# Attention scores of two heads on the two halves of TensorE's rows, in float32

## The chip, the cores and the metric

One core of one Trainium2 chip. The metric is the device time of one execution in microseconds; the kernel before is given by the median of three runs.

## The reference, cut to what matters

Per batch and head (B = 4, H = 8, S = 576, D = 64) a causal attention and a linear memory read are mixed by a gate; the result, 2304 tokens of 512 features, goes through two MLPs, all in float32.

```python
scores = q @ k.T / 8                     # causal
local = softmax(scores) @ v
phi = where(q > 0, q, exp(q) - 1) + 1
mem = (phi @ M_prev) / (phi @ z_prev + 1e-6)
x = g * mem + (1 - g) * local            # g = sigmoid(beta), per head
h = x @ w_in;  x = (h * sigmoid(1.702 * h)) @ w_out
h = x @ w_in2; x = (h * clip(h + 3, 0, 6) / 6) @ w_out2
```

## The kernel before, in words

**Work.** The tokens lie in six tiles of 384 (`TILES`, L73): the first 384 rows of one batch (g = 0), or the last 192 rows of two batches (g = 1), which attend to all 576 keys. Attention goes by pairs of heads, four a segment: 32 pairs, 16 of 384 rows (numbers 0 to 7 and 16 to 23) and 16 of 192 rows. The MLPs (`moe`, L271) hold their weights and the activations split into a float32r part and the rest, also float32r; each product is three full-array matmuls of 384 columns, and one tile takes 16 units of 24 matmuls.

**Stages.** The first tile's attention runs first, with the first weight pieces' conversion (`conv_w`, L188: weights come as float64 and are put together by DVE, POOL and ACT). Then the stream of the first MLP over tiles 0 to 4 has the attention of the next tile mixed in (`pump`, L800): `after_quarter` and the loop at L845 take one step of the attention generator whenever the MLP's count of quarter units passes a rate (L855). The rest of the conversion lies in tile 0's stretch (L854). Last come the first MLP's tile 5 and the whole second MLP without attention. The order on each engine's queue is set at build time by a scheduler from the order in which the code gives the instructions and a simulated timeline; each queue then runs in order. `Chains` (L87) hands out the follow-up steps of softmax, evacuation, gates and conversion one at a time.

**A pair.** `scores` (L464) writes the scores into PSUM banks; `soft` (L473) takes the masked minimum of the negated scores on DVE (L391), exponentials with sums on ACT (L396), the reciprocal on DVE and the scaling on POOL (L404). `turn` (L553) transposes the probabilities on PE and evacuates them. `mem_prep` and `mem_read` (L608, L626) make phi and the memory part. `weigh` (L663) forms the weighted sums with the values, each head on half of the array's columns (64 values' columns as weights), and adds the transposed memory part. Three PSUM banks (tag `a`) go round between all of them once the MLP runs; eight while the first tile's attention runs alone.

**How scores are formed.** Pairs 0 and 2 to 7 are not split: `product` (L436) multiplies float32 q and k, 64 rows of the array for one head, first head 0, then head 1. The others (`is_split`, L369) are split: `split_qk` (L422) loads q and k of one head twice, on both halves of the partitions, and makes the float32r part of q on POOL (L430), that of k on ACT (L431), q's rest on DVE (L433), k's rest on POOL or DVE (L434); the scores are then two full-array float32r matmuls per block. Blocks: 128, 256 and 384 columns a head in a 384-row pair (two banks a head), 512 columns in a 192-row pair; there the last 64 rows of both heads go together as the corner product (L517 to L522), 64x64 of the array each. A float32 matmul stands in the trace as two records (two passes), a transposition as one. In a 192-row pair the last block of sums (L690), the second memory block (L635) and its transposition (L696) use 64 rows or columns.

**Weighted sums of now**, with a step in the middle, at which the MLP can go on:

```python
av(0, lambda a: t[a][:, 0:384], 0, 384, 128, True)
yield
need(("t", i, 0, 1), ("t", i, 1, 1))
av(1, lambda a: t[a][:, 384:640], 128, 384, 128, False)
av(2, lambda a: t[a][:, 640:768], 256, 384, 128, False)
```

Of the kernel before, what the change touches and what calls it, by code (L numbers as in the profile page):

```python
# [8 lines left out]
F32 = mybir.dt.float32  # L9
# [15 lines left out]
KQ = 100  # L25
# [6 lines left out]
SPLIT = (2, 3, 4, 5)  # L32
SP0 = (1,)
KL0 = (1, 1)
SB = 1
RB = 3
T4B = 1
# [12 lines left out]
KLP = (1, 1, 1, 0, 0, 1)  # L50
# [20 lines left out]
GQK = 2 * N0  # L71
# [39 lines left out]
def attention_moe_kernel(ctx: ExitStack, tc: tile.TileContext, qk0, sk0, sk1, vm0, vm1, bb, w1, w2, out):  # L111
# [76 lines left out]
    def conv_w():  # L188

        key = layer, f, a = w_jobs[w_at[1]]  # L190
# [146 lines left out]
    banks = [3, 0]  # L337

    def bank(name):
        k = banks[1] % banks[0]  # L340
        banks[1] += 1
        if k < 3:
            return psa.tile([128, 512], F32, tag="a", bufs=3, name=name)
        return psy.tile([128, 512], F32, tag=("h", "y0", "y1", "y2", "y3")[k - 3], name=name)
# [6 lines left out]

    def at_transpose(*args):
        on_pe[:] = [PE.transpose(*args).ins]  # L353

    def attention(ap):
        qk, vm, pp, pt, phi, mo, raw, sp = {}, {}, {}, {}, {}, {}, {}, {}
        gens = {}
        norms, cut = [0, 0], set()
# [10 lines left out]
        def is_split(i):  # L369
            return pairs[i][0] in SPLIT or i in SP0  # L370

        def load_qk(i):
            if i >= NPAIR or is_split(i):
                return
            ti, si, b, g, p, _ = pairs[i]
            t = ap.tile([128, 2 * N0], F32, tag="raw", bufs=RB, name="qk")
            move(1, out=t[:, 0:GQK], in_=qk0[b, p])
            qk[i] = (t[:, 0:N0], t[:, N0:GQK])

# [15 lines left out]
        def expo(dst, o, m, s):  # L395
            ACT.activation(out=dst, in_=o, func=AF.Exp, scale=-1.0, bias=m, accum_out=s)  # L396
# [12 lines left out]
        def load_raw(i, a):  # L409
            if not 0 <= i < NPAIR or not is_split(i) or (i, a) in raw:  # L410
                return
            ti, si, b, g, p, _ = pairs[i]
            t = ap.tile([128, 2 * N0], F32, tag="raw", bufs=RB, name="raw")
            move(3, out=t, in_=(sk0, sk1)[g][b, 2 * p + a])
            raw[i, a] = t

        def split_start(i, a):
            if (i, a) in raw and (i, a) not in cut:
                cut.add((i, a))
                start(("sp", i, a), split_qk(i, a))  # L420

        def split_qk(i, a):  # L422
            ti, _, _, g = pairs[i][:4]
            nq, nk = ((N0, N0), (N1, S))[g]
            r = raw[i, a]
            t = ap.tile([128, 3 * N0], F32R, tag="sp", bufs=SB, name="sp")
            rq, rk = r[:, 0:nq], r[:, nq:nq + nk]
            q_h, q_l, ks = t[:, 0:nq], t[:, nq:2 * nq], t[:, 2 * nq:2 * nq + nk]
            sp[i, a] = q_h, q_l, ks
            POOL.tensor_scalar(out=q_h, in0=rq, scalar1=1.0, scalar2=1.0, op0=ALU.mult, op1=ALU.mult)  # L430
            ACT.copy(out=ks, in_=rk)  # L431
            yield
            DVE.tensor_tensor(out=q_l, in0=rq, in1=f32(q_h), op=ALU.subtract)  # L433
            (DVE, POOL)[KL0[a] if i < NP else KLP[ti]].tensor_tensor(out=ks[D:128], in0=rk[D:128], in1=f32(ks[D:128]), op=ALU.subtract)  # L434

        def product(i, a):  # L436

            ti, si, b, g, p, _ = pairs[i]
            if not is_split(i):
                q, k = qk[i]  # L440
                h = slice(64 * a, 64 * a + 64)

                def mm(o, c0):
                    n = o.shape[1]
                    at_matmul(o, lhsT=q[h, c0:c0 + 128], rhs=k[h, 0:n], start=True, stop=True)

                return mm, lambda: None

            split_start(i, a)
            need(("sp", i, a))  # L450
            q_h, q_l, ks = sp[i, a]

            def mm(o, c0):
                n = o.shape[1]
                at_matmul(o, lhsT=q_h[:, c0:c0 + 128], rhs=ks[:, 0:n], start=True, stop=False)
                at_matmul(o, lhsT=q_l[:, c0:c0 + 128], rhs=ks[:, 0:n], start=False, stop=True)

            def done():
                sp.pop((i, a))
                split_start(*((i, 1) if a == 0 else (i + 1, 0)))  # L460

            return mm, done

        def scores(i):  # L464
            ti, si, b, g, p, _ = pairs[i]
            norms[1] = ti
            if is_split(i):
                start(("p", i), mem_prep(i))
                load_raw(i + 1, 0)
            st = ap.tile([128, 12], F32, tag="st", name="st")  # L470
            mx, su = st[:, 0:6], st[:, 6:12]

            def soft(s, cols, a, dst, c):  # L473
# [7 lines left out]
                for x, (c0, c1) in enumerate(cols):  # L481
                    expo(dst[:, c0:c1], s[:, c0:c1], mx[:, c + x:c + x + 1], su[:, c + x:c + x + 1])
# [7 lines left out]
            for a in range(2):  # L490
                h = slice(64 * a, 64 * a + 64)
                mm, done = product(i, a)
                if g == 0:
                    t = ap.tile([128, 512], F32, tag="p", bufs=PB, name="p")
                    s = bank("s01")
                    mm(s[:, 0:128], 0)
                    mm(s[:, 128:384], 128)
# [429 lines left out]
```

## Time and profile before

| | us |
|---|---|
| median of three runs | 1102.02 (1100.32 to 1103.64) |
| the profiled execution | 1097.73 |
| its span | 1095.9 |
| PE busy | 1052.0 (96%) |
| DVE busy | 570.7 (52%) |
| ACT busy | 539.1 (49%) |
| POOL busy | 472.1 (43%) |
| granted clock of TensorE, mean | 0.984 |

PE is TensorE's matmul, PEld its weight load, DVE VectorE, ACT ScalarE, POOL GpSimd, SP the queue that issues DMAs. Matmuls are pipelined and a record is longer than the time until the next starts: what a matmul costs is read from start to start. "128*64" in a PE row are the array's rows and columns in use; the shape after it is the moving operand's. "L350" is the line of the helper that records every attention matmul, so the tile names (s scores, o sums, t transposes, mem memory) tell them apart. A wait "<- issue" is time in which the profile shows nothing that the engine waited for.

### The profile page before, as it was taken

How to read it: one execution, taken by the hardware profiler on the slowest of the kernel's cores; microseconds unless marked ns; L12 is line 12 of the kernel's file. 1: busy time of each engine (PE TensorE's matmuls, PEld its weight loads, DVE VectorE, ACT ScalarE, POOL GpSimd, SP SyncE). 2: the span in 40 equal slices, each digit the busy share in tenths (PEclk: the TensorE clock that was granted, in tenths of full speed). 3: DMA queues.
4: the chain of work that ended last, by engine and by line, in shares of the span. 5: the costliest groups of instructions: out<-in, count | busy, mean ns of one | idle time of the engine just before them, and what ended most of it. 6: DMA issues, size and time to landing. Idle time of an engine off the chain costs nothing.

```text
span 1095.9 us, 17060 instructions
## 1 busy us (share of the span) xinstructions
PE 1052.0 (96%) x6153; PEld 958.1 (87%) x6153; DVE 570.7 (52%) x1511; ACT 539.1 (49%) x1225; POOL 472.1 (43%) x526
## 2 busy tenths in 40 slices
PE   7988779999999999999999998998999999999998
PEld 5566667788889999889888997998999999999998
DVE  7899999635766564435445588884111121111210
ACT  6766665544555555435443566765233232332422
POOL 5688867544444435444543344543222222222221
PEclk9989989999999999999999998999999999999999
DMA  7542322212231212212120585101000010000000
GB/s 245 202 184 101 121 82 63 73 58 74 82 106 54 63 40 82 69 48 73 44 63 25 204 294 176 57 1 44 15 29 30 1 59 1 30 29 1 30 1 29
DMA packets 32627, 81.77 MB, mean 75 GB/s; under 512 B 3744, under 2 KB 12960, under 8 KB 32544
## 3 DMA queue, kind: packets, MB, share of 16 engines
q1 hardware_dynamic: 32544, 80.69, 21.9%
q8 instruction: 48, 0.79, 0.3%
q14 instruction: 35, 0.29, 0.1%
HBM read 71.24 MB, written 9.44 MB: 74 GB/s over the span
## 4 chain that ended last, share of the span: by engine, by line
PE 76%; DVE 11%; issue 6%; POOL 5%; ACT 1%; DMA 1%; SPq 0%; POOLq 0%; ACTq 0%; DVEq 0%
PE h L305 10%; PE h L307 10%; PE h L306 10%; PE y L287 10%; PE y L286 10%; PE y L285 10%; PE o L350 6%; PE s L350 5%; PE t L353 3%; POOL r L209 2%; POOL g L268 2%; DVE r L205 2%; DVE r L200 2%; PE mem L350 1%; DVE s L391 1%
## 5 line engine op out<-in xcount | busy, mean ns | idle before, releaser
L268 POOL TENSOR_TENSOR g<-t,g 128x384 fp32r<-128x384 f32 x176 | 183.5, 1043 | 407.7 <-ACT g L266 380.9
L305 PE MATMUL h<-xs,w 128*128 128x384 f32 x768 | 266.9, 348 | 19.8 <-DVE t L259 12.3
L306 PE MATMUL h<-xs,w 128*128 128x384 f32 x768 | 261.1, 340 | 0.3 <-DVE w L228 0.3
L307 PE MATMUL h<-xs,w 128*128 128x384 f32 x768 | 261.1, 340 | 0.3 <-DVE xs L251 0.2
L285 PE MATMUL y<-g,w 128*128 128x384 f32 x768 | 259.1, 338 | 0.6 <-ACT g L266 0.5
L286 PE MATMUL y<-g,w 128*128 128x384 f32 x768 | 257.4, 336 | 0.0
L287 PE MATMUL y<-g,w 128*128 128x384 f32 x768 | 241.4, 339 | 3.1 <-DVE g L268 2.9
L263 DVE SCALAR_TENSOR_TENSOR t<-t,h 128x384 f32<-128x384 f32 x96 | 53.1, 553 | 272.1 <-ACT t L261 272.1
L305 PEld LDWEIGHTS h<-xs,w 128*128 128x128 f32 x768 | 147.2, 192 | 30.3 <-DVE t L259 16.7
L266 ACT CAST g<-t 128x384 fp32r<-128x384 f32 x192 | 98.5, 513 | 111.6 <-DVE t L259 56.8
L287 PEld LDWEIGHTS y<-g,w 128*128 128x128 f32 x768 | 141.4, 188 | 9.1 <-DVE g L268 3.9
L307 PEld LDWEIGHTS h<-xs,w 128*128 128x128 f32 x768 | 146.8, 191 | 1.6 <-DVE xs L251 1.1
L306 PEld LDWEIGHTS h<-xs,w 128*128 128x128 f32 x768 | 147.2, 192 | 1.1 <-DVE w L228 0.6
L285 PEld LDWEIGHTS y<-g,w 128*128 128x128 f32 x768 | 144.7, 188 | 3.2 <-issue 1.0
L286 PEld LDWEIGHTS y<-g,w 128*128 128x128 f32 x768 | 144.5, 188 | 0.3
L261 ACT ACTIVATE t<-h,three 128x384 f32<-128x384 f32 x96 | 55.6, 579 | 169.6 <-PE h L307 169.6
L404 POOL TENSOR_SCALAR p<-p,st,omg 128x128 f32<-128x128 f32 (+2 forms) x128 | 93.4, 737 | 84.3 <-DVE st L400 58.7
L391 DVE CUSTOM_DVE_ANT_0 s<-s,mask 128x128 f32<-128x128 f32 (+2 forms) x144 | 73.8, 519 | 74.7 <-PE s L350 73.5
L396 ACT ACTIVATE p<-s,st 128x128 f32<-128x128 f32 (+3 forms) x160 | 82.9, 524 | 25.7 <-DVE st L391 23.3
L259 DVE SCALAR_TENSOR_TENSOR t<-t,h 128x384 f32<-128x384 f32 x96 | 52.7, 549 | 62.1 <-ACT t L257 59.0
L257 ACT ACTIVATE t<-h 128x384 f32<-128x384 f32 x96 | 47.0, 490 | 61.6 <-PE h L307 54.4
L209 POOL TENSOR_SCALAR r<-r 128x512 f32<-128x512 f32 x64 | 57.1, 895 | 30.5 <-DVE r L205 22.4
(86 smaller groups left out, 1348.2 us busy)
## 6 DMA issues: line engine op xcount, KB each, us to landing
r<-in_w_dram SPq DMA_DIRECT2D x64, 512.0 KB, 5.0
raw<-in_sk_dram SPq DMA_DIRECT2D x50, 384.0 KB, 3.2
vm<-in_vm_dram SPq DMA_DIRECT2D x16, 386.0 KB, 3.0
x2d<-yo SPq DMA_DIRECT2D x24, 192.0 KB, 2.0
xr<-x2d SPq DMA_DIRECT2D x24, 192.0 KB, 3.1
out_dram<-yo SPq DMA_DIRECT2D x24, 192.0 KB, 1.9
vm<-in_vm_dram SPq DMA_DIRECT2D x16, 258.0 KB, 2.8
qk<-in_qk_dram SPq DMA_DIRECT2D x7, 384.0 KB, 3.8
```

The source lines that it names most:

```text
L266: gated["ACT"].append(ACT.copy(out=g[:, 0], in_=t).ins)
L268: d = (DVE, POOL)[GLE[ti if layer == 0 else -1]].tensor_tensor(out=g[:, 1], in0=t, in1=f32(g[:, 0]), op=ALU.subtract)
L285: PE.matmul(ys[d], lhsT=w[:, 0, o:o + 128], rhs=g[:, 0], start=(f == 0), stop=False)
L286: PE.matmul(ys[d], lhsT=w[:, 1, o:o + 128], rhs=g[:, 0], start=False, stop=False)
L287: PE.matmul(ys[d], lhsT=w[:, 0, o:o + 128], rhs=g[:, 1], start=False, stop=(f == NF - 1))
L305: PE.matmul(h, lhsT=w[:, 0, c:c + 128], rhs=x[:, 0], start=(kk == 0), stop=False)
L306: PE.matmul(h, lhsT=w[:, 1, c:c + 128], rhs=x[:, 0], start=False, stop=False)
L307: PE.matmul(h, lhsT=w[:, 0, c:c + 128], rhs=x[:, 1], start=False, stop=(kk == KD - 1))
L350: on_pe[:] = [PE.matmul(out, **args).ins]
L391: DVE.tensor_tensor_reduce(out=o, in0=o, in1=m, scale=-SCALE, scalar=init, op0=ALU.add, op1=ALU.min, accum_out=out)
L396: ACT.activation(out=dst, in_=o, func=AF.Exp, scale=-1.0, bias=m, accum_out=s)
L404: (DVE, POOL)[e[norms[0] % len(e)]].tensor_scalar(out=dst, in0=dst, scalar1=s, scalar2=w, op0=ALU.mult, op1=ALU.mult)
```

## The change

Both heads' scores are formed from float32 q and k for all pairs, head 0 on rows 0 to 63 of the array and head 1 on rows 64 to 127, into two banks, block by block in turns. The matmuls of a bank pair are tied in order, and the first of them is given all waits: for the last readers of both banks (`in_a_run`, `free`, `has_read`). The split of q and k goes, with its buffers and loads; for 192-row pairs each head loads its 64 partitions with a DMA of its own. The weighted sums of a pair, with the memory part's transpositions, become one such run, which waits for all evacuated transposes and the scaled memory part; the step in the middle goes. In 192-row pairs the 64-row remainders are padded to 128: `t4` has zero rows, and the second memory block is rows 64 to 191, whose first 64 get the weight zero (`gall`'s fourth block). A weight piece first finishes the piece four before it. Steps per pair fall from 12 to 9 and from 9.5 to about 7; the rates `KQ` and those in `pump` are set to that.

```diff
-KQ = 100
+KQ = 80
-SPLIT = (2, 3, 4, 5)
-SP0 = (1,)
-SB = 1
+GW = (0, 2)
...
     def conv_w():
-        key = layer, f, a = w_jobs[w_at[1]]
+        n = w_at[1]
+        key = layer, f, a = w_jobs[n]
+        if n >= 4 and w_jobs[n - 4] in w_gen:
+            chains.finish(w_gen[w_jobs[n - 4]])
...
+    def after(ins, deps):
+        for dep in deps:
+            tc.add_manual_dep(
+                ins, dep.name, mybir.DependencyInfo(mybir.DependencyClass.Sync, mybir.DependencyReason.DATA),
+                reason="one run of matmuls",
+            )
+
+    def in_a_run(deps):
+        run = []
+        def mm(out, **args):
+            ins = PE.matmul(out, **args).ins
+            if run:
+                tc.add_manual_dep(
+                    ins, run[-1].name,
+                    mybir.DependencyInfo(mybir.DependencyClass.NoSync, mybir.DependencyReason.DATA),
+                    reason="one run of matmuls",
+                )
+            else:
+                after(ins, deps)
+            run.append(ins)
+            on_pe[:] = [ins]
+        return mm
...
+        t4 = ap.tile([128, 2, 64], F32, tag="t4", bufs=1, name="t4")
+        POOL.memset(t4, 0.0)
...
         def load_qk(i):
-            if i >= NPAIR or is_split(i):
+            if i >= NPAIR:
                 return
...
+            if g == 0:
+                move(1, out=t, in_=qk0[b, p])
+                qk[i] = (t[:, 0:N0], t[:, N0:2 * N0])
+            else:
+                for a in range(2):
+                    h = slice(64 * a, 64 * a + 64)
+                    move(3, out=t[h], in_=sk1[b, 2 * p + a][h])
+                qk[i] = (t[:, 0:N1], t[:, N1:N1 + S])
...
-        def split_qk(i, a):
...
         def scores(i):
+            def product(banks, blocks):
+                mm = in_a_run(free(banks[0]) + free(banks[1]))
+                for o0, o1, c0 in blocks:
+                    for a in range(2):
+                        h = slice(64 * a, 64 * a + 64)
+                        mm(
+                            banks[a][:, o0:o1], lhsT=q[h, c0:c0 + 128], rhs=k[h, 0:o1 - o0], start=True, stop=True
+                        )
...
+            if g == 0:
+                parts = (((0, 128, 0), (128, 384, 128)), ((0, 384, 256),))
+            else:
+                parts = (((0, 512, 0),),)
...
+            for x, blocks in enumerate(parts):
+                s = [bank("s") for _ in range(2)]
+                product(s, blocks)
+                for a in range(2):
+                    gen = soft(s[a], [(o0, o1) for o0, o1, _ in blocks], a, t[a][x], c + 3 * a if g == 0 else a)
+                    start(("s", i, a, x), gen)
+                c += len(blocks)
                 yield
...
         def rows(g):
-            return ((0, 128), (128, 128), (256, 128)) if g == 0 else ((0, 128), (128, 64))
+            return (0, 128, 256) if g == 0 else (0, N1 - 128)
...
         def mem_prep(i):
-            for h, r in q:
-                ACT.activation(out=e[h, 0:n], in_=r, func=AF.Exp)
+            ACT.activation(out=e[:, 0:n], in_=r, func=AF.Exp)
...
         def weigh(i):
+            need(("t", i, 0, 0), ("t", i, 0, 1), ("t", i, 1, 0), ("t", i, 1, 1), ("m", i))
             o = bank("o")
+            mm = in_a_run(list(made.pop(i).values()))
...
+                av(0, lambda a: t[a][:, 0:384], 0, 384, True)
+                av(1, lambda a: t[a][:, 384:640], 128, 384, False)
+                av(2, lambda a: t[a][:, 640:768], 256, 384, False)
             else:
                 for j in range(4):
-                    av(j, lambda a: t[a][:, j], 0, N1, 128, j == 0)
-                    if j == 1:
-                        yield
-                av(4, lambda a: t[2][:, a], 128, N1, 64, False)
+                    av(j, lambda a: t[a][:, j], 0, N1, j == 0)
+                av(4, lambda a: t4[:, a], 128, N1, False)
...
         def gates():
+            POOL.memset(gall[0:64, 3], 0.0)
+            ACT.copy(out=gall[:, 1:3], in_=gall[:, 0:1].to_broadcast([128, 2, H]))
+            ACT.copy(out=gall[64:128, 3], in_=gall[64:128, 0])
...
-                pump((qi - OFF) / (PG0 * 128 / 48 if TILES[ti + 1][0][1] == 0 else PG1 * 128 / 76))
+                pump((qi - OFF) / (PG0 * 128 / 36 if TILES[ti + 1][0][1] == 0 else PG1 * 128 / 57))
```

## Rows read from the trace of the kernel before

**Rows 1.** The page, part 4: chain that ended last, shares of the span by engine.
```profile
PE 76%; DVE 11%; issue 6%; POOL 5%; ACT 1%; DMA 1%; SPq 0%; POOLq 0%; ACTq 0%; DVEq 0%
```
**Rows 2.** Busy time of each engine by stage; the row names its columns.
```profile
core 0: us, PE busy (x) PEld busy (x) DVE busy (x) ACT busy (x) POOL busy (x), PEclk, DMA share, GB/s
0.00:14.00 14.00, 7.72 (x32) 6.43 (x33) 7.85 (x31) 6.94 (x19) 5.94 (x16) 0.90 0.84 300
14.00:57.00 43.00, 41.03 (x208) 23.66 (x207) 38.52 (x161) 32.11 (x99) 28.65 (x39) 0.98 0.59 208
57.00:192.00 135.00, 112.95 (x604) 94.52 (x605) 132.89 (x287) 87.04 (x189) 106.59 (x100) 0.92 0.30 105
192.00:609.00 417.00, 415.37 (x2600) 362.27 (x2601) 220.60 (x767) 208.53 (x539) 181.37 (x228) 1.00 0.21 63
609.00:1096.00 487.00, 474.98 (x2716) 471.28 (x2714) 170.81 (x269) 204.52 (x381) 149.59 (x145) 0.99 0.17 58
```
**Rows 3.** Timeline of PE, third stage: start us, us, engine, line, operation, count.
```profile
302.71 0.33 PE L286 MATMUL y<-g,w 128*128 128x384 f32 x1
302.88 0.34 PE L285 MATMUL y<-g,w 128*128 128x384 f32 x1
303.15 0.87 PE L350 MATMUL o<-pt,vm 128*64 128x192 f32 x8
303.95 0.62 PE L350 MATMUL s<-sp 128*128 128x384 f32 x2
304.50 0.55 PE L350 MATMUL o<-pt,vm 128*64 128x192 f32 x4
```
**Rows 4.** Timeline of PE, second stage: one head's float32 scores on half the rows.
```profile
63.00 0.91 PE L350 MATMUL s<-qk 64*128 64x384 f32 x2
63.84 0.33 PE L350 MATMUL o<-ident,mo 128*128 128x128 f32 x1
```
**Rows 5.** Timeline of PE, third stage: both heads' scores of the corner.
```profile
244.86 1.19 PE L350 MATMUL s<-raw 64*64 64x512 f32 x8
245.99 0.55 PE L353 MATMUL t4a<-ident,p 128*128 128x128 f32 x3
```
**Rows 6.** Groups by line on DVE, 57 to 192 us (busy us, mean ns | idle before).
```profile
L433 DVE TENSOR_TENSOR sp<-raw,sp 128x192 fp32r<-128x192 f32 x8 | 8.1, 1018 | 0.0
L624 DVE SCALAR_TENSOR_TENSOR phi<-raw,phi 64x192 f32<-64x192 f32 x6 | 3.7, 610 | 0.1
```
**Rows 7.** Groups by line on POOL, 57 to 192 us.
```profile
L434 POOL TENSOR_TENSOR sp<-raw,sp 64x576 fp32r<-64x576 f32 x8 | 13.1, 1642 | 0.7
L430 POOL TENSOR_SCALAR sp<-raw 128x192 fp32r<-128x192 f32 x8 | 4.1, 516 | 1.9 <-PE s L350 1.9
```
**Rows 8.** Waits, whole span: us in total, times, longest us.
```profile
PEld o L350 <- issue: 23.8, 103, 0.5
PEld s L350 <- issue: 14.9, 59, 0.6
```
**Rows 9.** Timeline of POOL and PE, first stage: pair 1's split and its scores.
```profile
9.34 0.51 POOL L430 TENSOR_SCALAR sp<-raw 128x384 fp32r<-128x384 f32 x1 [7.29 <-DMA raw<-in_sk_dram]
...
11.35 1.86 PE L350 MATMUL s<-sp 128*128 128x128 f32 x6 [4.96 <-POOL sp L434]
```
**Rows 10.** Groups by line on DVE, 192 to 609 us.
```profile
L433 DVE TENSOR_TENSOR sp<-raw,sp 128x192 fp32r<-128x192 f32 (+1 forms) x40 | 20.3, 507 | 1.8 <-POOL sp L430 1.3
```
**Rows 11.** Timeline of DVE and ACT, third stage: softmax of one head's scores.
```profile
239.56 0.70 DVE L391 CUSTOM_DVE_ANT_0 s<-s,mask 128x512 f32<-128x512 f32 x1 [1.22 <-PE s L350]
...
240.18 0.14 DVE L391 DVE_READ_ACCUMULATOR2_ANT st<- 128x1 f32 x1
...
240.35 0.69 ACT L396 ACTIVATE p<-s,st 128x512 f32<-128x512 f32 x1
```
**Rows 12.** Waits of PE, first 192 to 609 us, then 57 to 192 us.
```profile
PE h L305 <- DVE t L259: 1.3, 2, 1.0
...
PE h L305 <- DVE t L259: 11.0, 5, 4.3
```

More of the change, by code (lines that the diff above doesn't have):

```diff
@@ L70 @@
 BIG = 3.4028234e38
-GQK = 2 * N0
 MZ = 132
@@ L336, in attention_moe_kernel @@
     NPAIR = len(pairs)
-    banks = [3, 0]
+    banks = [3, 0, 0]
+    place = {}
+    last_read = {}
     def bank(name):
@@ L342, in bank, with has_read, free @@
         if k < 3:
-            return psa.tile([128, 512], F32, tag="a", bufs=3, name=name)
-        return psy.tile([128, 512], F32, tag=("h", "y0", "y1", "y2", "y3")[k - 3], name=name)
+            t = psa.tile([128, 512], F32, tag="a", bufs=3, name=name)
+            at = ("a", banks[2] % 3)
+            banks[2] += 1
+        else:
+            tag = ("h", "y0", "y1", "y2", "y3")[k - 3]
+            t = psy.tile([128, 512], F32, tag=tag, name=name)
+            at = (tag, 0)
+        place[id(t)] = at, t
+        return t
+    def has_read(t, d):
+        last_read[place.pop(id(t))[0]] = d.ins
+    def free(t):
+        d = last_read.get(place[id(t)][0])
+        return [] if d is None else [d]
     on_pe = []
@@ L395, in expo @@
         def expo(dst, o, m, s):
-            ACT.activation(out=dst, in_=o, func=AF.Exp, scale=-1.0, bias=m, accum_out=s)
+            return ACT.activation(out=dst, in_=o, func=AF.Exp, scale=-1.0, bias=m, accum_out=s)
         def inverse(s):
@@ L407, in norm @@
             norms[0] += 1
[L409 to L420, printed above, removed]
-        def split_qk(i, a):
[L423 to L431, printed above, removed]
-            yield
[L433 to L462, printed above, removed]
         def scores(i):
@@ L539, in scores, with evac @@
                 yield
-            if is_split(i):
-                need(("p", i))
-                load_raw(i + 1, 1)
-        def evac(jobs):
+        def evac(i, jobs):
             yield
-            for e, out, in_ in jobs:
+            for e, out, in_, *bank_done in jobs:
                 if e is ACT:
-                    ACT.copy(out=out, in_=in_)
+                    d = ACT.copy(out=out, in_=in_)
                 else:
-                    DVE.tensor_copy(out=out, in_=in_)
+                    d = DVE.tensor_copy(out=out, in_=in_)
+                made.setdefault(i, {})[e] = d.ins
+                for t in bank_done:
+                    has_read(t, d)
         def turn(i):
@@ L707, in split @@
                 if XEV[i % len(XEV)]:
-                    DVE.tensor_copy(out=x[:, c:c + n], in_=o[:, 0:n])
+                    d = DVE.tensor_copy(out=x[:, c:c + n], in_=o[:, 0:n])
                 else:
-                    ACT.copy(out=x[:, c:c + n], in_=o[:, 0:n])
+                    d = ACT.copy(out=x[:, c:c + n], in_=o[:, 0:n])
+                has_read(o, d)
             start(("x", i), split())
@@ L726, in attention @@
             load_qk(k)
-            for a in range(2):
-                load_raw(k, a)
             if k == 0:
@@ L745, in attention @@
             if has(i):
-                if not is_split(i):
-                    start(("p", i), mem_prep(i))
+                start(("p", i), mem_prep(i))
                 load_qk(i + 2)
-                if has(i + 1) and is_split(i + 1) and not is_split(i):
-                    for a in range(2):
-                        load_raw(i + 1, a)
             if has(i - 2) and pairs[i - 2][5]:
```

137 lines of the change are left out of this document (47 added, 90 removed).

## The prediction

> **What bounds the kernel now.** I read the table by stage first, then the chain, then PE's timeline at single runs of matmuls, then the queue that is full in each stage. The chain that ended last is 76% PE and 11% DVE [rows 1]; one number for a span with three regimes, so the stages decide [rows 2]. From 0 to 57 us the first tile's attention runs alone: DVE is busy 46.4 of 57 us, PE 48.8. From 57 to 192 us the first tile's MLP, the second tile's attention and the weight conversion run together: DVE is busy 132.9 of 135 us and PE only 113.0, so **DVE bounds this stage**. From 192 to 609 us four MLP tiles run with the rest of the attention: PE 415.4 of 417 us, DVE 220.6: **PE bounds it**. From 609 us on only MLP is left; the change touches nothing there, and I cost those 487 us at no change.
>
> In the third stage the MLP needs 4 x 384 matmuls, which follow each other every 0.17 us (0.1735 over a longer stretch) [rows 3]: 266 us. So 150 us are attention. Its column work by the code, at two columns' time per fp32 pass, two passes (one in a transposition) and 2.4 GHz: a 384-row pair 4.8 us, a 192-row pair 5.2 us. Of the 16 pairs of 192 rows, a quarter's splits lie in the second stage already (8 of 32 instructions, see part 1); counting 13 here, and 8 of 384 rows, makes 106 us. The rest, some 44 us, is above all the price of going into and out of matmuls that use a part of the array. One such run: the MLP matmul at 302.88 holds PE 0.27 instead of 0.17 us before the weighted sums start; those (eight records of 192 columns, two heads side by side: 4 x 0.16 = 0.64 us) take 0.80; then a first full-array matmul pays about 0.1 more [rows 3]. In and out: **0.36 us per run of weighted sums**. For fp32 scores on one half of the rows: 0.84 us where the columns need 0.64 [rows 4], with 0.1 on either side: **0.40 us per run**. The split scores of now are full-array float32r matmuls and pay none of this between MLP matmuls.
>
> **Part 1, scores from float32.** Column time first. Split: two matmuls per head of one column time each; float32: two passes per head of two, but both heads at once if the halves of the rows work side by side. A 384-row pair: 2 x 2 x 768 columns = 4 x 768 = 1.28 us, both ways; a 192-row pair's 512 columns: 0.85 both ways. So split pairs save no columns; the seven unsplit ones (0, 2 to 7), whose heads run one after the other now, halve from 2.56 to 1.28 us.
> Do the halves overlap? No row shows two 64-row matmuls with 128 output columns at once. Nearest: the 64x64 corner pair, both heads, 512 and 64 columns, takes 1.13 us to the next matmul, where overlapped columns need 0.96 and serial ones 1.92 [rows 5]; and the sums on the array's column halves [rows 3]. Both overlap fully, so I take full overlap; serial is the other bound (1.28 and 0.85 us more a pair) and a rival.
> The Trainium skill ("TensorE: Matmul & The Clock Gate", Part 3) measured 3.07 times for four row tiles, not four; two tiles at that efficiency would make a pair's scores some 0.39 and 0.26 us dearer, about 6 us over the third stage (an estimate from that page). The corner pair shows no such loss [rows 5].
> What goes with the split: on DVE the subtraction L433 (8 in the second stage, 8.1 us) and half of phi's instructions L624 (6 of 0.61 us become 3) [rows 6]; on POOL L434 and L430 (13.1 + 4.1 us) [rows 7]; on ACT a cast per head. In the third stage DVE, ACT and POOL have half their time free, so there this is worth nothing.
>
> **Part 2, weighted sums in one run, padded.** By the code a 384-row pair's sums are two runs now, one after. A 192-row pair now leaves full-array mode up to six times: two runs of sums, the 64-row block of sums (another mode), the 64-column memory block, its 64-row transposition, and the corner scores; about 2.0 us with those that touch each other. After: scores, corner scores, sums: 0.40 + 0.36 + 0.36 + 0.05 for a transposition of 128 columns instead of 64 = 1.17 us. That 162 entries into partial modes are seen as drains now (103 and 59) [rows 8] against 96 runs after (64 of scores, 32 of sums) says the same.
>
> **Sum by stage.**
> *0 to 57 us.* Pair 1's scores start at 11.35, held 4.96 us by POOL's split, which began when the halves had landed at 9.34 [rows 9]; without it about 2 us earlier. On PE five unsplit pairs are scored here: 5 x 1.28 = 6.4; ten runs fewer, 4.0; four runs of sums fewer, 1.4; pair 1's two new runs, 0.8 back: 11 us. DVE caps that: it idles 10.6 us, most of it before the first scores exist, and loses about 2 us of work. I take **-6** (bounds -2 and -12).
> *57 to 192 us.* DVE loses 8.1 + 1.8 + some 0.8 of 64-row memory instructions = 10.7 us. Besides, DVE runs slowly here: L433 took 1018 ns, against 507 in the third stage [rows 6, 10], while POOL was busy 106.6 of 135 us [rows 2]. With 17.2 us of POOL work gone I add 4 us (16% of some 25 us lost that way over the conversion's instructions; an estimate). **-15** (bounds -3, if other DVE work moves in, and -24). PE's need there, about 105 us, isn't reached.
> The Trainium skill ("SBUF — State Buffer", Who interferes with whom) says that DVE and POOL take a shared port in turns, the loser fully blocked; by that all 17.2 us of POOL could come back on DVE and the stage give -28 at the most. The doubled L433 agrees in kind; how much each POOL instruction blocks no row tells.
> *192 to 609 us.* 13 pairs of 192 rows: 2.0 - 1.17 = 0.83 each, -10.8. Eight of 384 rows: two runs (0.72) become three (1.16): +3.5. **-8** (-7.3 rounded up, since short waits inside today's broken runs go too; bounds -18, if half of the unexplained 44 us went, and with serial halves 8 x 1.28 + 13 x 0.85 = 21 more, +13).
> *Costed at nothing.* Loads: a pair's q and k are 384 KB instead of twice that, as one DMA or two halves on SP's queue, issued two pairs ahead; DMA is 21% busy in the third stage. The memset on POOL and the small copies on ACT at the start lie under the first loads. That a weight piece first finishes the one four before: pieces start 3.75 steps apart and take six, so two are under way, and it doesn't bite; if it did, DVE's stage would feel it. Pacing (12 steps a 384-row pair become 9, 9.5 a 192-row pair about 7) keeps attention's share of a tile.
> Total -29. The profiled execution took 1097.73 us (span 1095.9), 4.3 below the median of the runs: 1097.7 - 29 = 1068.7, in terms of the median **1073**.
>
> **New waits.** The first matmul of a run waits for everything the run needs: two free banks of the three, or all four evacuated transposes and the scaled memory part. PE's queue is in order, so the MLP matmuls behind it, then gates, then everything, wait too.
>
> **Rivals.** (a) *Slower: bank waits.* One head's softmax holds its bank for DVE 0.70 and 0.14 and ACT 0.69 us [rows 11]; the second head's is freed some 0.85 later. If each of the third stage's 42 score runs waits that 0.85 and each of the 21 runs of sums 0.35 for its last evacuation, 43 us come on top: 1116. It decides from a mean wait of 29/63 = 0.46 us per run. For: three banks, two taken at once. Against: PE waits for an engine only 1.3 us for DVE in that stage now [rows 12], and between two score runs lie about three steps, 3 us of MLP and attention work. (b) *The halves don't overlap.* +21 in the third stage, +6 in the first: 1073 + 27 = 1100, no change. For: no row shows it; against: the two overlaps that are seen [rows 3, 5]. (c) *DVE's stage keeps its length*, since ACT, POOL and the conversion chain take turns or later attention is pulled in: -3 instead of -15, 1085. For: attention of the third tile already runs in it; PE waited 11.0 us there for the gate's DVE step, behind conversion [rows 12].
>
> **Numbers.** Forecast 0.60, (c) 0.20, (a) 0.12, (b) 0.08. A measurement of this kernel tells about 0.3%, 3.3 us, from no change. Faster: forecast, (c) and a little of (b): 0.82; same: 0.06; slower: 0.12. The range reaches from all three stages near their good bounds, 1051, over (c) to just short of (b), 1096; what is left out is (a) and most of (b), 0.2.
>
> **What would show it.** Stage one ends near 51 us with pair 1's scores at about 9; stage two lasts near 120 us, DVE still full; in stage three four MLP tiles and attention take near 409 us. The two heads' score matmuls start within 10 ns of each other, and a 384-column run of both takes about 0.84 us to the next. Entries seen as drains fall to about 100. Wrong would be: PE waiting for ACT's exp or evacuation ahead of runs (a), score records following one another at full length (b), an unshortened second stage (c).

## The result, and the profile after

The changed kernel takes **1083.54 us** (median of 4 runs, 1082.27 to 1084.36), beside 1101.17 for the kernel before (1097.98 to 1103.64, 4 runs): ratio 0.9848, 95% interval 0.9829 to 0.9867. That is 17.6 us less where 29 were forecast; 1083.5 lies inside the range and next to the 1085 of rival (c). The two profiled executions differ by less, 1097.73 to 1084.36, since the one of before is among its fastest runs and the one of after is its slowest; what follows locates those 13.4 us of span, and the last four by medians have no place in a trace.

Busy time of each engine by stage, columns as in [rows 2], but with borders at the same work in both kernels: the first matmul of the first MLP, the first one of tile 1's MLP, and the seventh unit of tile 5's MLP, behind the last attention. First before, then after.

```profile
0.00:55.95 55.95, 47.69 (x235) 29.03 (x235) 45.32 (x190) 39.04 (x118) 33.54 (x53) 0.97 0.64 227
55.95:197.01 141.06, 117.72 (x634) 97.90 (x633) 138.89 (x298) 89.82 (x196) 110.45 (x104) 0.92 0.31 106
197.01:632.25 435.24, 434.90 (x2706) 383.18 (x2707) 230.47 (x782) 218.32 (x558) 188.09 (x235) 1.00 0.23 74
632.25:1095.90 463.65, 451.73 (x2581) 448.03 (x2580) 156.00 (x246) 191.95 (x355) 140.06 (x136) 0.99 0.14 47
```

```profile
0.00:50.15 50.15, 38.11 (x231) 23.68 (x231) 40.45 (x181) 35.18 (x114) 27.15 (x51) 0.92 0.61 219
50.15:187.61 137.46, 115.00 (x634) 94.03 (x633) 128.07 (x286) 86.15 (x190) 97.26 (x87) 0.90 0.32 108
187.61:616.85 429.24, 426.88 (x2712) 372.85 (x2712) 184.31 (x659) 184.90 (x495) 130.67 (x169) 1.00 0.18 53
616.85:1082.50 465.65, 453.40 (x2581) 449.77 (x2580) 157.40 (x249) 192.60 (x357) 144.01 (x139) 0.99 0.14 50
```

Stage one is 5.8 us shorter (forecast 6), stage two 3.6 (forecast 15), stage three 6.0 (forecast 8), the last 2.0 longer (forecast 0). The second stage is the surprise: DVE's busy time there fell by 10.8 us, but its share of the stage went from 98% to 93%. What PE did not get is in the third number: its idle time, 141.06 - 117.72 = 23.3 us before, is 137.46 - 115.00 = 22.5 after. The waits of PE between these borders show what it is made of (us in total, times, longest us), first the gate step's of before, then the largest of after:

```profile
PE h L305 <- DVE t L259: 12.0, 6, 4.3
```

```profile
PE h L302 <- DVE t L256: 7.5, 6, 2.3
PE s L381 <- issue: 3.5, 1, 3.5
PE t L396 <- DVE mo L640: 2.9, 1, 2.9
PE s L381 <- DVE mo L640: 2.8, 1, 2.8
PE h L302 <- DVE st L449: 2.1, 1, 2.1
```

The gate step is waited for 4.5 us less. In its place stand waits for the scaled memory part (DVE, `mo`), of which before has none in this stage: 5.7 us by name, and the 3.5 us "<- issue", of a score run that starts 0.1 us after the last step on `mo` has ended; by its time it is the same wait, though the profile does not name it. That makes 9.2 us. The memory part's bank is one of the three that go round, and the next score run or transposition wants it. Two of them in the timeline: DVE does conversion steps between the memory part's own steps (L635 to L640), 6.3 and 3.5 us from the first to the end of the last.

```profile
77.49 0.15 DVE L635 TENSOR_SCALAR mw<-mem 128x6 f32<-128x6 f32 x1
...
83.09 0.67 DVE L640 TENSOR_TENSOR mo<-mem,mw 128x128 f32<-128x128 f32 x3
...
83.86 1.65 PE L381 MATMUL s<-qk 64*128 64x128 f32 x8 [3.50 <-issue]
...
160.59 0.14 DVE L635 TENSOR_SCALAR mw<-mem 128x4 f32<-128x4 f32 x1
160.65 0.68 DVE L215 SCALAR_TENSOR_TENSOR wt<-r 128x512 f32<-128x512 f32 x1
...
163.58 0.49 DVE L640 TENSOR_TENSOR mo<-mem,mw 128x128 f32<-128x128 f32 x2
...
164.21 0.63 PE L396 MATMUL t<-ident,p 128*128 128x128 f32 x4 [2.94 <-DVE mo L640]
```

The granted clock of the stage is 0.92 before and 0.90 after. Read as time at 1.2 GHz beside 2.4 GHz these means are some 23 and 27 us (an estimate), so a small part of what the stage did not gain may lie there.

The array's halves do overlap. Both heads' 384 columns in the third stage, to the next matmul, take 0.84 us; one head alone took that in [rows 4]:

```profile
388.30 0.92 PE L381 MATMUL s<-qk 64*128 64x384 f32 x4
389.14 0.44 PE L302 MATMUL h<-xs,w 128*128 128x384 f32 x1
```

Pair 1's scores, at 11.35 in [rows 9], start at 9.17 now, and what they wait for is their load:

```profile
9.17 0.93 PE L381 MATMUL s<-qk 64*128 64x128 f32 x8 [3.08 <-DMA qk<-in_qk_dram]
```

### The profile page after: what moved, and what is told of

It is laid out like the page before. It is cut to its first block, busy times and chain, and to the rows that moved or that the text cites. A ratio compares the mean times of both kernels' runs of the same rounds, so it can differ in the third digit from the quotient of the medians.

```text
span 1082.5 us, 16719 instructions
## 1 busy us (share of the span) xinstructions
PE 1033.4 (95%) x6153; PEld 940.3 (87%) x6153; DVE 510.2 (47%) x1372; ACT 498.8 (46%) x1152; POOL 399.1 (37%) x444
## 5 line engine op out<-in xcount | busy, mean ns | idle before, releaser
L263 ACT CAST g<-t 128x384 fp32r<-128x384 f32 x192 | 98.4, 513 | 95.1 <-DVE t L260 49.2
L454 POOL TENSOR_SCALAR p<-p,st,omg 128x128 f32<-128x128 f32 (+3 forms) x128 | 91.8, 729 | 99.3 <-DVE st L450 44.7
L446 ACT ACTIVATE p<-s,st 128x256 f32<-128x256 f32 (+4 forms) x160 | 82.4, 521 | 69.6 <-DVE st L441 57.5
L441 DVE CUSTOM_DVE_ANT_0 s<-s,mask 128x128 f32<-128x128 f32 (+3 forms) x144 | 72.6, 526 | 85.0 <-PE s L381 84.1
L381 PE MATMUL s<-qk 64*128 64x256 f32 (+5 forms) x384 | 72.3, 466 | 12.2 <-issue 3.5
```

The lines of the kernel that those rows point to most:

```text
L263: gated["ACT"].append(ACT.copy(out=g[:, 0], in_=t).ins)
L381: ins = PE.matmul(out, **args).ins
L441: DVE.tensor_tensor_reduce(out=o, in0=o, in1=m, scale=-SCALE, scalar=init, op0=ALU.add, op1=ALU.min, accum_out=out)
L446: return ACT.activation(out=dst, in_=o, func=AF.Exp, scale=-1.0, bias=m, accum_out=s)
L454: (DVE, POOL)[e[norms[0] % len(e)]].tensor_scalar(out=dst, in0=dst, scalar1=s, scalar2=w, op0=ALU.mult, op1=ALU.mult)
```

## The experiments

Each kernel is compared with the kernel before on the same chip, so ratios are what is compared (0.001 is 1.1 us). The stage lengths in the table are read at the three borders above in each kernel's trace; "PE idle" is stage two less PE's busy time in it, "DVE" its busy time there, "matmuls" PE's records there (24 of the 658 of "heads in turn" come from blocks that are cut in two).

| kernel | median us | ratio (95%) | one | two | three | last | PE idle | DVE | matmuls |
|---|---|---|---|---|---|---|---|---|---|
| before | | 1 | 56.0 | 141.1 | 435.2 | 463.7 | 23.3 | 138.9 | 634 |
| after | 1083.54 | 0.9848 (.9829 to .9867) | 50.2 | 137.5 | 429.2 | 465.6 | 22.5 | 128.1 | 634 |
| sums only | 1083.34 | 0.9864 (.9849 to .9879) | 52.2 | 139.4 | 423.7 | 466.0 | 26.3 | 135.8 | 606 |
| scores only | 1095.78 | 0.9972 (.9958 to .9986) | 49.8 | 132.9 | 445.7 | 463.9 | 23.1 | 125.8 | 603 |
| sums in two parts | 1082.90 | 0.9862 (.9847 to .9877) | 49.9 | 133.3 | 434.2 | 463.9 | 24.8 | 126.6 | 606 |
| two parts, after's pace | 1089.87 | 0.9909 (.9895 to .9924) | 49.8 | 145.4 | 426.9 | 465.9 | 24.9 | 127.5 | 647 |
| pieces free | 1088.81 | 0.9910 (.9889 to .9931) | 49.9 | 136.1 | 435.4 | 464.8 | 24.8 | 127.6 | 602 |
| step on ACT | 1083.41 | 0.9862 (.9847 to .9877) | 49.3 | 131.7 | 432.8 | 466.3 | 21.4 | 119.1 | 608 |
| heads in turn | 1086.38 | 0.9894 (.9878 to .9910) | 49.2 | 138.9 | 430.5 | 465.8 | 26.2 | 129.6 | 658 |
| split 3, 4 | 1079.55 | 0.9829 (.9814 to .9843) | 49.6 | 137.2 | 423.8 | 466.2 | 22.8 | 128.0 | 634 |
| **split 3, 4, 5** | **1074.47** | **0.9778** (.9764 to .9793) | 49.2 | 137.4 | 419.5 | 464.6 | 22.8 | 128.2 | 635 |
| split 3, 4, 5, step on ACT | 1073.22 | 0.9773 (.9757 to .9789) | 49.8 | 131.7 | 422.8 | 466.2 | 21.7 | 118.8 | 608 |
| split 3, 4, 5, two parts early | 1077.69 | 0.9798 (.9782 to .9814) | 51.6 | 133.5 | 425.0 | 466.1 | 22.9 | 126.6 | 602 |
| the same, step on ACT | 1075.23 | 0.9781 (.9767 to .9796) | 51.2 | 131.2 | 425.1 | 466.1 | 22.1 | 116.6 | 603 |

The theory after the result: the weighted sums bring the gain, the scores bring theirs in stage one and cost in stage three, and a shorter stage two comes back later. The rivals: DVE or the pieces' order still holds stage two, or the halves overlap only in part.

**Each half of the change alone.** "Sums only" is the kernel before with the weighted sums, their padding and their single run of after; scores are split as before.

```diff
-        gens = {}
+        gens, made = {}, {}
...
-                    at_matmul(
-                        o[h, c0:c1], lhsT=v[0:kr, j, h], rhs=rhs(a), start=first, stop=False, skip_group_check=True
-                    )
+                    mm(o[h, c0:c1], lhsT=v[:, j, h], rhs=rhs(a), start=first, stop=False, skip_group_check=True)
...
-                pump((qi - OFF) / (PG0 * 128 / 48 if TILES[ti + 1][0][1] == 0 else PG1 * 128 / 76))
+                pump((qi - OFF) / (PG0 * 128 / 44 if TILES[ti + 1][0][1] == 0 else PG1 * 128 / 68))
```

> The kernel before with the second part of the change alone: weighted sums of a pair in one run and the 64-row remainders padded; scores stay split and unsplit as before (KQ 95, the rates in pump 44 and 68, for one step less a pair). By the prediction's prices (0.36 us a run of sums, 0.40 a run of float32 scores) the sums save in the third stage 13 x 1.2 + 8 x 0.36 = 19 us and the float32 scores cost 8 x 0.8 + 13 x 0.4 = 12 of it again, so this kernel should be near 1080 to 1084, level with the changed one, its third stage the shorter of the two by about 10 us and its first two stages the longer. Rival: the scores are what pays (no splits to wait for between the matmuls) and the sums alone bring under 8 us: 1093 or more.

Measured: 1083.34, the same as both parts together and inside its range; its third stage is 5.5 us shorter than after's, where 10 were expected. "Scores only" is the kernel after with the sums of before:

```diff
                 mm(
-                    o[:, r0:r0 + 128], lhsT=m[:, k * 128:(k + 1) * 128], rhs=ident, is_transpose=True,
+                    o[:, r0:r0 + nr], lhsT=m[0:nr, k * 128:(k + 1) * 128], rhs=ident[0:nr, 0:nr], is_transpose=True,
...
-                av(4, lambda a: t4[:, a], 128, N1, False)
+                av(4, lambda a: t4[0:64, a], 128, N1, False, 64)
```

> The kernel after with float32 scores, and the weighted sums as before: issued in two parts, 64-row blocks not padded, pace 40 and 65. Theory (scores earn in stages one and two and cost in stage three; padding is what the sums part still earns without the tie): stage one about 6 us shorter, stage two 4 to 8 us shorter, stage three 8 to 12 us longer than the kernel with two padded parts; total 1088 to 1094 at a before of 1098.6. Rival one (padding is worth nothing, it is only the pace of the steps): 1082 to 1085. Rival two (float32 scores are worth nothing alone): 1096 to 1100.

Measured: ratio 0.9972, 3.1 us gained; the median, 1095.78, lies above the theory's range and just below that of rival two. The stage lengths carry the theory's signs: -6.2, -8.2, +10.5 against before. But stage two holds 31 matmuls fewer than before and stage three 35 more, so the second and third numbers are in part one thing, moved:

```profile
49.80:182.68 132.88, 109.82 (x603) 89.18 (x603) 125.75 (x278) 84.00 (x184) 97.80 (x88) 0.94 0.32 108
182.68:628.37 445.69, 441.06 (x2741) 376.78 (x2741) 194.69 (x723) 187.59 (x503) 136.13 (x173) 1.00 0.17 55
```

Taken together the two stages are 2.3 us longer (578.6 for 576.3). So float32 scores save 6 us while attention runs alone and lose some 2 beside the MLP; the sums save 13.2 beside it (563.1) and 3.7 in stage one. The two ratios multiplied, 0.9972 x 0.9864 = 0.9836, are the 0.9848 of both within its interval: the halves just add.

**Which part of the sums.** "Sums in two parts" is the kernel after with the padding, but without the tie to all four transposes and with the step in the middle again, pace 40 and 65 instead of 36 and 57.

```diff
-            need(("t", i, 0, 0), ("t", i, 0, 1), ("t", i, 1, 0), ("t", i, 1, 1), ("m", i))
...
-            mm = in_a_run(list(made.pop(i).values()))
+            mm = at_matmul
...
                 for j in range(4):
                     av(j, lambda a: t[a][:, j], 0, N1, j == 0)
+                    if j == 1:
+                        yield
```

> The kernel after with the weighted sums issued in two parts again without the tie to all four transposes, padding to 128 columns kept, pace of the steps raised from 36 and 57 to 40 and 65. Theory of a price per run: one run of sums more for each pair, 21 pairs in stage three and 11 ahead, at 0.36 us: 7.5 and up to 4 us more, 1089 to 1095. Rival one (padding of 64 columns to 128 pays, the tie does not): 1082 to 1085. Rival two (the tie's waits cost what it saves): 1078 to 1082.

Measured: 0.9862, rival one. Against scores only, which differs in the padding alone, that is 0.0110 or 12 us: **the padding is what pays**. The unpadded end of a 192-row pair's sums changes the array's form twice more (`64*64`, then a transposition over 64 rows). The sums of one pair in an unbroken run, up to the next MLP matmul, in scores only, in sums in two parts and in after take 2.17, 1.76 and 1.75 us:

```profile
235.04 1.52 PE L366 MATMUL o<-pt,vm 128*64 128x192 f32 x16
236.49 0.33 PE L366 MATMUL o<-t,vm 64*64 64x64 f32 x4
236.75 0.53 PE L366 MATMUL o<-ident,mo 128*128 128x128 f32 x2
237.21 0.44 PE L302 MATMUL h<-xs,w 128*128 128x384 f32 x1
```

```profile
231.57 1.52 PE L366 MATMUL o<-pt,vm 128*64 128x192 f32 x16
...
233.33 0.42 PE L302 MATMUL h<-xs,w 128*128 128x384 f32 x1
```

```profile
597.10 1.52 PE L381 MATMUL o<-pt,vm 128*64 128x192 f32 x16
...
598.85 0.42 PE L302 MATMUL h<-xs,w 128*128 128x384 f32 x1
```

So the step in the middle does not always part a pair. Where it does, as here in sums in two parts, the sums take 1.45 + 0.78 = 2.23 us, 0.48 more:

```profile
211.97 1.51 PE L366 MATMUL o<-pt,vm 128*64 128x192 f32 x14
213.42 0.44 PE L302 MATMUL h<-xs,w 128*128 128x384 f32 x1
...
217.56 0.38 PE L366 MATMUL o<-pt,vm 128*64 128x192 f32 x1
...
218.34 0.42 PE L282 MATMUL y<-g,w 128*128 128x384 f32 x1
```

That is not the price of one more run alone: a block has four records, and after 14 the cut goes through one, so that its two heads no longer run side by side. Over the last 23 pairs the sums' runs, each read from its first start to the next matmul that is none of them, add up to 44.8 us in two parts and 43.9 in after. Without the tie 8 of the 23 pairs ran unbroken anyway, with it 20, and a run that is followed by float32 scores takes some 1.92 us. So the tie saves about 1 us of the sums' own time, where 7.5 and more were expected. That stage three is 5.0 us shorter in after is work moved (634 matmuls in stage two for 606; stages two and three together take 566.7 and 567.5). Does the tie still gain or lose something elsewhere, which the pace that was set with it hides?

```diff
-                pump((qi - OFF) / (PG0 * 128 / 40 if TILES[ti + 1][0][1] == 0 else PG1 * 128 / 65))
+                pump((qi - OFF) / (PG0 * 128 / 36 if TILES[ti + 1][0][1] == 0 else PG1 * 128 / 57))
```

> The kernel with two padded parts, at the pace of the kernel after (36 and 57): the two differ then in the tie alone. Theory (the tie makes PE wait in stage two for the scaled memory part and saves about 5 us of mode changes in stage three): stage two still near 133 us, stage three near 434, total 1081 to 1085. Rival (the pace made stage two shorter, not the tie): stage two 137 or more, total 1087 to 1092.

Measured: 0.9909, stage two 145.4: the rival, the pace. At one pace the two kernels differ by 0.0061, 6.7 us; with the pace set to them, two parts cost nothing. By the code (`before_h`) the steps that are left over are all taken ahead of the tile's last unit; that two parts leave more over, and that this lengthens the stage, is argued from it and not traced. So the tie, with its step less a pair, is worth 6.7 us or nothing, by what the pace is.

**What sets stage two.** First the order of the pieces: without the rule that a piece first finishes the one four before. This one changes the computation: a piece can overwrite a temporary that the piece four before it has still to read, so some weights are not the reference's.

```diff
-        if n >= 4 and w_jobs[n - 4] in w_gen:
-            chains.finish(w_gen[w_jobs[n - 4]])
```

> The changed kernel without the rule that a weight piece first finishes the one four before it. If the rule costs nothing, as the prediction said, the time stays within 3 us of the changed kernel (1080 to 1087). If it holds the conversion up and so took back the second stage's gain, that stage gets 5 to 10 us shorter: 1074 to 1079.

Measured: stage two 136.1 instead of 137.5, with 32 matmuls fewer in it, and 0.9910 in all, some 7 us slower than after and above both ranges; why it is slower, no run shows. The rule does not hold the stage up. Then DVE itself: one of its conversion steps moved to ACT in that stage.

```diff
-ABS = ((0, 2), (1, 2), (2, 2))
+ABS = ((0, 2), (2, 2), (2, 2))
```

> The changed kernel with every weight piece's absolute value on ACT (ABS (2, 2) in place of (1, 2) for the second stage's pieces), which takes some 17 instructions, 9.6 us, from DVE there and gives ACT 0.69 us for each. If DVE's work still sets the length of the second stage, it gets 6 to 9 us shorter: 1075 to 1078. If the chain of a piece through DVE, POOL and ACT or the matmuls' waits set it, nothing is gained: 1081 to 1088.

Measured: DVE's work in stage two falls by 9 us, the stage by 5.8, the third grows by 3.6, the total does not move (0.9862 beside 0.9848): the second range.

```profile
49.30:180.99 131.69, 110.29 (x608) 90.95 (x606) 119.10 (x263) 90.82 (x198) 92.19 (x86) 0.91 0.34 113
180.99:613.81 432.82, 429.94 (x2739) 375.12 (x2737) 187.94 (x670) 185.98 (x498) 130.84 (x170) 1.00 0.17 53
```

PE's records say what happened: 608 for 634 in stage two, 2739 for 2712 in stage three. Attention of the third tile, which fills stage two's end, was not reached and runs later, where PE is full. Across all fourteen kernels PE's idle time in stage two lies between 21.4 and 26.3 us, while DVE's work runs from 116.6 to 138.9: **what would have to shrink is PE's idle time, and unloading DVE by some 20 us took 1 or 2 off it.** Nor is it one wait: the waits behind `mo` are 9.2 us in after and 5.4 in sums in two parts (two score runs "<- issue" that start 0.1 us after `mo`), whose stage is as idle with 24.8 us. They came with the scores of both heads at once, which want two banks, and not with the tie: the two kernels that score one head after the other, before and sums only, have none there.

**Do the halves overlap because the blocks alternate?** Here head 0's blocks are all issued ahead of head 1's, tied in that order; the largest blocks are cut in two.

```diff
-                for o0, o1, c0 in blocks:
-                    for a in range(2):
-                        h = slice(64 * a, 64 * a + 64)
+                for a in range(2):
+                    h = slice(64 * a, 64 * a + 64)
+                    for (o0, o1, c0), k0 in zip(blocks, ks):
```

> The changed kernel with the two heads' score matmuls in the order of heads, two blocks of one head and then two of the other (the 384 and 512 column blocks halved for it), so that at most the second block of head 0 and the first of head 1 can overlap. If the halves of the rows work side by side, a 384-row pair's scores take 0.21 + 0.32 us longer and a 192-row pair's 0.43: about 10 us in the third stage, 1092 to 1096. If they never overlapped, the order makes no difference: 1082 to 1086.

Measured: 0.9894, some 5 us slower than after and between the two ranges, but not for want of overlap; where the 5 us come from stays open. The two blocks of 128 and 256 columns for both heads, eight records, in the third stage: the run by 381.10 and by 381.35 (with the shape of all four records), then in full by shapes, and the matmul behind it:

```profile
381.08 0.39 PE L381 MATMUL s<-qk 64*128 64x128 f32 x2
L381 PE MATMUL s<-qk x4: 272/322/373, 381.1 to 381.3; 64*128 64x128 f32 x4
L381 PE MATMUL s<-qk x8: 272/374/378, 381.1 to 381.6; 64*128 64x128 f32 x4, 64*128 64x256 f32 x4
381.94 0.33 PE L396 MATMUL t<-ident,p 128*128 128x128 f32 x1
```

0.86 us to the next matmul; one after the other 2 heads x 384 columns x 2 passes x 2 / 2.4 GHz would be 1.28 (an estimate). Two records have started by 381.10, and the first four are all of 128 columns: by the code's order a 256-column block of head 0 stands between the two blocks of 128. So head 1's first block starts ahead of head 0's second, which was issued earlier. The order of the heads does not switch the overlap off, and a serial version could not be tried this way.

**Float32 scores only where they earn.** Scores only gains in stage one and loses beside the MLP; so the kernel after, with the split scores of before for the attention of tiles 3, 4 and 5 (sums as in after) and the pace there set to the steps, 44 and 68:

```diff
+SPLIT = (3, 4, 5)
...
-            q, k = qk[i]
+            if is_split(i):
+                start(("p", i), mem_prep(i))
+                load_raw(i + 1, 0)
+                q = k = None
+            else:
+                q, k = qk[i]
```

> Left as in the kernel after for tiles 0 to 2 (float32 scores); scores split again for the attention of tiles 3, 4 and 5, weighted sums in one run and padded everywhere. Theory: the price of a float32 score run is paid where PE is full, the saving of its columns is made where both heads ran one after the other (stage one), and DVE's relief only matters in stage two. By the two traces, the kernel after had gained about 16 us against before when the third tile's MLP began, and the kernel with the sums alone gained about 11 us from there on: together some 25 us, 1075 to 1079 at a before of 1099 to 1101 (ratio 0.978 to 0.981). In stage three the PE time of MLP beside runs falls back by some 5 us. Rival one (gains overlap, since less attention is left for the later tiles whichever way it was done earlier): 1081 to 1084, same as after. Rival two (split work of GpSimd and VectorE in the third stage makes PE wait): 1085 and over.

Measured: **1074.47, 0.9778**, faster than both kernels and just under the range that was expected for adding gains (1075 to 1079). Stage three is 9.7 us shorter than after's with the same number of matmuls (x2713 for x2712), and DVE's extra 35 us do not hold PE up there (it waits 0.5 us for a step of DVE):

```profile
49.15:186.55 137.40, 114.64 (x635) 93.61 (x633) 128.24 (x286) 86.04 (x190) 97.47 (x87) 0.91 0.32 107
186.55:606.07 419.52, 416.93 (x2713) 382.35 (x2712) 218.91 (x723) 210.26 (x543) 170.95 (x217) 1.00 0.22 69
```

With tiles 3 and 4 alone, the eight 384-row pairs:

```diff
-SPLIT = (3, 4, 5)
+SPLIT = (3, 4)
```

> Like the run before, but only tiles 3 and 4 (the eight 384-row pairs of the third stage) split again. Theory of the price per run: a 384-row pair has two score runs at 0.40 us, so eight pairs give back 6.4 us at the predicted price, 1077 at an after of 1083.5; at the price that the traces give (the whole of float32 scores cost some 5.5 us in stage three, for 21 pairs) 8/21 to 16/42 of it, 2 to 3 us: 1080 to 1082. Rival (only the last attention tile, 192-row pairs, is where float32 scores cost): no change against after.

Measured: 0.9829, 2 us under after (the intervals overlap), 5.6 us over the kernel with tile 5 split too. In all, 24 score runs given back (two a pair in tiles 3 and 4, one in the eight pairs of tile 5), with the pace set for it, are worth 0.0070, 7.7 us: 0.32 us each, where 0.40 was forecast. That is a mean: the medians give 2 us to the 16 runs of tiles 3 and 4 and 5.6 to the eight of tile 5, stage three of the traces 5.4 and 4.3. One price for both kinds is not shown.

The next three ask whether stage two's relief adds to this, with the step on ACT, with sums in two parts for tiles 0 and 1, and with both:

```diff
-            mm = in_a_run(list(made.pop(i).values()))
+            mm = in_a_run(d) if tie else at_matmul
```

> Tiles 3 to 5 split as in the first run, and stage two's first conversion step on ScalarE instead of VectorE. Theory (VectorE sets stage two's length, but what is saved there is attention that is not pulled in and runs later): stage two about 132 us, third stage longer by the same 3 us, total within 3 us of the first run. Rival (in the run with ScalarE alone the gain was lost by chance of the order later on): 3 to 6 us under the first run.

> Scores split again for tiles 3 to 5, sums in one run only from tile 2 on; tiles 0 and 1 with two padded parts (pace 40 and 65 there). Theory (the tie costs some 4 us in stages one and two and saves some 5 us in stage three): 1069 to 1072, stage two near 133 us. Rival (what the two parts gain in stage two is attention of the third tile done later, and comes back): 1073 to 1076, as with the tie everywhere.

> The run before with stage two's first conversion step on ScalarE as well. Theory: VectorE sets stage two's length and both relieve the same stage, so they don't add: within 2 us of the run before, stage two near 130 us. Rival (they add): 3 to 6 us less than the run before.

Measured: 0.9773, 0.9798 and 0.9781. Each shortens stage two by 4 to 6 us and gives 3 to 6 back in stage three, as the theory of moved work says; two parts early also lose 2 us in stage one, and the kernel ends 2 us over the one with the tie everywhere, against its theory and above its rival's range. Step and two parts together gain 0.0017 over two parts alone (2 us), less than the 3 to 6 by which they would add.

## Why the prediction was right, and where it was not

**Sign, stage one: right.** 5.8 us for 6. It starts as said (pair 1's scores at 9.17, "about 9") and ends as said, with PE busy 38.11 us for 47.69 and DVE 40.45 for 45.32: PE was spared 9.6 us and the stage gave less, in line with the cap by DVE, which no run tests alone.

**Stage two, -15: this is the step that failed.** DVE's busy time fell by 10.8 us where 10.7 of work and 4 of relief from POOL were costed, and the relief is there:

```profile
L265 DVE TENSOR_TENSOR g<-t,g 128x384 fp32r<-128x384 f32 x15 | 11.1, 739 | 0.0
```

```profile
L268 DVE TENSOR_TENSOR g<-t,g 128x384 fp32r<-128x384 f32 x15 | 14.8, 986 | 0.0
```

(columns busy us, mean ns, idle; after, then before, second stage by its earlier borders.) The same 15 gate products take 247 ns less each, 3.7 us, and a conversion step (L202) takes 909 ns for 971; but 29 of those lie in the stage for 27, so that DVE got other work in place of some that it was spared. The Trainium skill ("SBUF — State Buffer", Who interferes with whom) has an instruction of DVE with two inputs in SBUF contend with POOL's reads. These rows agree in kind (POOL's busy time fell from 110.5 to 97.3 us), and the upper bound of -28, an estimate from that page, was far off.

What failed is the inference "DVE is busy 98% of the stage, so the stage shrinks by what DVE is spared". The stage ends when PE has gone through what lies in its queue, and PE's idle time came out the same: its waits for the gate step shrank, and new waits for a bank behind the scaled memory part took their place. Of the 22.5 us some 19 are still waits for single steps of DVE (7.5 + 3.5 + 2.9 + 2.8 + 2.1): PE was held up by when these steps came in DVE's queue, and sparing DVE work did not bring them sooner. The new waits were named under "New waits" (two free banks of the three), and priced only as rival (a), in stage three. The fall in length that other kernels show in this stage is work put off: matmuls in the stage fall with it. So **rival (c) came true**, in part by the road it said: no later attention was pulled in (634 matmuls both times), but PE waits for DVE's steps behind conversion. Its -6 - 3 - 8 = -17 is what the medians show; the traces show 13.4, so that its total fits so well is in part luck.

**Stage three, -8: the net is right (-6.0), its two terms were both too large.** That the net came out is in part luck. Scores as costed were +8 x 0.80 + 13 x 0.40 = 11.6 us, 0.40 a run; splitting tiles 3 to 5 again gives 0.32 a run, pace and all. The sums side was then 19 us; sums only shows 13.2 in stages two and three together. The place of it was half wrong: 0.36 us for each run saved was forecast for both kinds of pairs alike, and the runs show some 12 us for padding, in 192-row pairs alone, and between nothing and 7 for the single run, of whose own time the tie saves about 1.

**Rival (b), the halves' overlap: rightly held to be unlikely.** Both heads take the 0.84 us of one. At the efficiency of packed row tiles in the Trainium skill ("TensorE: Matmul & The Clock Gate", Part 3) it would have been some 6 us dearer over stage three, an estimate. The row shows no such loss. **Rival (a)** did not come in stage three, where PE's longest sum of waits for another engine is 0.8 us:

```profile
PE t L396 <- ACT p L446: 0.8, 1, 0.8
```

Its mechanism showed in stage two. **The drains** were to fall to about 100. The waits "<- issue" of scores and sums are 76 and 75, for 59 and 103 [rows 8]: 151. So one of them does not stand for one run, and the agreement of 162 with the count of runs was no support.

**The last stage, costed at nothing, is 2.0 us longer** with the same 2581 matmuls. About half arises where the second MLP begins. The other half lies behind it, where after has a stretch of 3.4 us at 1.2 GHz that before has not; the same ten us behind the border, before and after:

```profile
750.40:760.40 10.00, 7.92 (x43) 7.10 (x42) 4.73 (x8) 5.81 (x13) 4.15 (x4) 1.00 0.26 80
```

```profile
735.00:745.00 10.00, 8.04 (x37) 7.41 (x36) 5.72 (x10) 6.04 (x13) 3.35 (x4) 0.83 0.25 79
```

Six matmuls fewer are about 1 us. Why the clock fell here only, and what sets the first half, stays open: the kernels' 463.7 to 466.3 us go neither with the pace (463.9 at 40 and 65, 465.9 at 36 and 57 without the tie) nor with the form of the scores.

**What stays open** besides: what would take PE's 22 us of idle time out of stage two. No run tried a fourth bank there, or the memory part's DVE steps ahead of conversion.

## What to carry to other kernels

An engine that is busy 98% of a stage bounds it only if the others' idle time shrinks when it is relieved: look at the next engine's waits, and count its instructions between two fixed points of the work, before a shorter stage is called a gain. What the code ties into one run may run unbroken without the tie: count the runs in the trace before a price is put on each. Where a stage overlaps a stream that is paced by steps, a change that alters the number of steps is compared at a pace of its own. A price per change of the array's form is worth paying only where it buys something: float32 on half the rows halves the columns of unsplit heads where PE works alone, and buys nothing beside full-array matmuls; padding a 64-row remainder to the form of its neighbours did better than anything else here.

## What was not expected of the hardware

Matmuls on the two row halves ran side by side although they were issued head after head: by the widths, head 1's block of 128 columns starts within 20 ns of head 0's, ahead of head 0's block of 256 that stands before it in the code's order, and all eight records take 0.86 us instead of 1.28. The Trainium skill ("TensorE: Matmul & The Clock Gate", Part 3) has matmuls start and end in program order. For starts on different row halves this run speaks against it, though its records do not name the head, only the widths tell, and the order is that of the code.
